# From the third batch on, q times k^T v as four plain float32 matmuls, one per quadrant of the array

## The chip, the cores and the metric

The kernel runs on one core of a Trainium2 chip. The time is device microseconds of one execution. The core has a matmul engine (PE in the rows, with its weight loads as PEld), a vector engine (DVE), a scalar engine (ACT), a general engine (POOL) and a queue that issues the transfers (SP). Each engine works through its own instructions in program order.

## What is computed

Eight batches of linear attention with eight heads, an RMS norm over each head, and a feed-forward block with a SiLU gate on all tokens:

```python
kv  = np.einsum('bhsd,bhse->bhde', k, v)          # 64 x 64 for each head
out = np.einsum('bhsd,bhde->bhse', q, kv)
rms = np.sqrt(np.mean(out * out, axis=-1, keepdims=True) + 1e-06)
x   = (out / rms * g_norm)                        # 4608 tokens x 512
h   = x @ w_in                                    # 512 x 2048
y   = (h * (1.0 / (1.0 + np.exp(-h)))) @ w_out    # 2048 x 512
```

Batch 8, heads 8, sequence 576, head dimension 64, everything in float32.

## The kernel before

The feed-forward block is nearly all the work. It runs over nine tiles of 512 tokens. Each operand there is split into an upper part that the array takes whole (type `fp32r`) and the rest, and a product is three matmuls: lower times upper, upper times lower, upper times upper. Tiles 0 and 1 are plain; from tile 2 on seven block products take the place of eight, for which sums of weight blocks are made on the way, written to DRAM and loaded back each step (`load_sums`, tile `wi<-sums_in_dram`).

Attention of batch b is woven into the feed-forward steps of earlier tiles. A batch is four pairs of heads (`Pair`), so 128 partitions hold two heads of 64. The place of every piece is written out by hand: `STAGES[b]` gives, in thirds of a step, when a pair's k and v are loaded (`load_kv`), when k^T v is made (`kv`), when q is loaded, split, multiplied (`out`, two thirds per pair: one for each half of its 576 columns), summed, scaled and kept. Third n belongs to step n // 3 and to its first, middle or last jobs by n % 3. Since every engine keeps program order, this list is also the order on each engine.

For a pair, `split_q` makes `qh` (ACT, L396) and `ql` (POOL, L401) out of `q`. All these tiles, with k and v, come from one pool of eight buffers (`kvq`), so a load of the next batch waits until an older tile of the ring is released. k^T v of the four pairs stands in one bank; `upper_kv` (ACT) copies it to `kh` and `lower_kv` (DVE) puts the rest in `kl`, both block-diagonal with zeros outside, so that one 128 x 128 weight tile serves both heads. `mm_out` then makes one half of the columns, 256 or 320 of them, by three matmuls (L414, L415, L416) in one bank. The banks for this are two, taken in turn (`at_bank`, tags `at` and `other`). `copy_out` empties a bank by two ACT instructions: the square (L420) and the scaled copy (L421).

The sums of weight blocks for the seven products are made between these: `make_sums` adds and subtracts on DVE (L691, L694), casts on ACT (L699), subtracts on POOL (L700) and stores. `move_a22` is one more ACT copy (L746). `spread` and `scale` of the batch before are on DVE (L434, L442).

Of the kernel before, what the change touches and what calls it, by code (L numbers as in the profile page):

```python
# [8 lines left out]
F32 = mybir.dt.float32  # L9
F32R = mybir.dt.float32r  # L10
# [29 lines left out]
        "load_q": (42, 42, 42, 48),  # L40
        "upper": 42,
        "lower": 43,
        "split": (46, 51, 54, 57),
        "out": (52, 53, 55, 56, 58, 59, 61, 62),
        "sums": (54, 57, 62, 63),
        "root": ((63, 6), (64, 5), (65, 3), (66, 4)),
# [6 lines left out]
        "load_q": (66, 66, 66, 72),  # L53
        "upper": 66,
        "lower": 66,
        "split": (70, 73, 76, 79),
        "out": (76, 77, 78, 80, 82, 83, 85, 86),
        "sums": (78, 81, 85, 87),
        "root": ((88, 6), (89, 4), (89, 4), (90, 4)),
# [6 lines left out]
        "load_q": (91, 93, 93, 99),  # L66
        "upper": 91,
        "lower": 92,
        "split": (97, 98, 103, 106),
        "out": (101, 102, 104, 105, 107, 108, 110, 111),  # L70
        "sums": (103, 106, 109, 112),
        "root": ((112, 6), (114, 4), (115, 4), (116, 4)),
# [6 lines left out]
        "load_q": (114, 114, 114, 120),  # L79
        "upper": 114,  # L80
        "lower": 115,
        "split": (118, 118, 121, 127),
        "out": (124, 125, 127, 129, 131, 132, 134, 135),
        "sums": (126, 129, 132, 135),
        "root": ((136, 7), (138, 4), (139, 4), (140, 3)),
# [6 lines left out]
        "load_q": (138, 138, 138, 144),  # L92
        "upper": 138,
        "lower": 139,
        "split": (142, 145, 148, 151),
        "out": (148, 149, 151, 152, 154, 155, 157, 158),
        "sums": (151, 154, 157, 160),
        "root": ((160, 6), (161, 4), (162, 4), (163, 4)),
# [6 lines left out]
        "load_q": (162, 162, 162, 168),  # L105
        "upper": 162,
        "lower": 163,
        "split": (166, 171, 172, 175),
        "out": (172, 173, 175, 176, 178, 179, 181, 182),
        "sums": (174, 177, 180, 183),  # L110
        "root": ((187, 7), (188, 4), (189, 3), (190, 4)),
# [20 lines left out]
def linear_attention_rms_silu_ffn(  # L132
# [22 lines left out]
    nc = tc.nc  # L155
    B, NP, P, S = q.shape
    D = P // 2
# [11 lines left out]
    const = ctx.enter_context(tc.tile_pool(name="const", bufs=1))  # L169
# [14 lines left out]
    def gap(pool, size, name):  # L184
        pool.tile([P, size // 4], F32, name=name, bufs=1)
# [8 lines left out]
    gap(const, 128, "gap_first")  # L194
    gap(tmp, 192, "gap_tmp")
    gap(gp, 64, "gap_gated")
    kh, kl = (const.tile([P, NP, P], F32R, name=name) for name in ("kh", "kl"))
    ident = weights.tile([P, P], F32, name="ident", tag=f"wo{EARLY}")
    make_identity(nc, ident)
    first_kv = weights.tile([P, NP * P], F32, name="first_kv", tag=f"wo{EARLY - 1}")  # L200
# [151 lines left out]
    def newton(y, u, m, eps=0.0):  # L352
# [4 lines left out]
            lambda: nc.vector.scalar_tensor_tensor(out=y, in0=u, scalar=1.5, in1=y, op0=ALU.add, op1=ALU.mult),  # L357
        ]

    class Pair:  # L360


# [24 lines left out]
        def split_q(self):  # L387

            self.qh = kvq.tile([P, S], F32R, name="qh", tag="kvq")
            self.ql = kvq.tile([P, S], F32R, name="ql", tag="kvq")  # L390
            cols = slice(0, S)
            if self.b == 1:
                cols, most = slice(TN, S), slice(0, TN)
                bank = h_bank() if self.c else at_bank()
                nc.scalar.copy(out=bank, in_=self.q[:, most])
            nc.scalar.copy(out=self.qh, in_=self.q)  # L396
            if self.b == 1:
                nc.vector.tensor_tensor(
                    out=self.ql[:, most], in0=bank, in1=self.qh[:, most].bitcast(F32), op=ALU.subtract
                )  # L400
            nc.gpsimd.tensor_tensor(  # L401
                out=self.ql[:, cols], in0=self.q[:, cols], in1=self.qh[:, cols].bitcast(F32), op=ALU.subtract
            )

        def begin_out(self):
            self.sq = tmp.tile([P, S], F32, name="sq", tag="tmp")
            self.o = opool.tile([P, S], F32, name="o")
# [49 lines left out]
    class FirstPair(Pair):  # L457
# [10 lines left out]
        def copy_kv(self):  # L468
            for h in range(2):
                d = slice(h * D, (h + 1) * D)  # L470
                nc.scalar.copy(out=kvm[self.c][d, d], in_=self.kv[h])
# [124 lines left out]
    def h_bank():  # L596
        return ps_h.tile([P, 512], F32, name="hp", tag="h")
# [6 lines left out]
    def at_bank(tag=None):  # L604

        at_tags.append(at_tags.pop(0))
        return ps_at.tile([P, 512], F32, name="at", tag=tag or at_tags[-1])
# [32 lines left out]
    def sums_of(t):  # L640

        whole, half = slice(0, DM), (slice(0, DM // 2), slice(DM // 2, DM))
        banks = [(acc_bank(), n, whole) for n in range(TN // P)]
        if t == NT - 1:
            last, n, _ = banks.pop()
            banks += [(last, n, half[0]), (at_bank(), n, half[1])]
        return banks
# [632 lines left out]
    def at(jobs, step, *calls):  # L1280
        jobs.setdefault(step, []).extend(calls)

    def at_third(n, *calls):
        at((first_jobs, mid_jobs, last_jobs)[n % 3], n // 3, *calls)

    def spread_at(make, *places):

        calls = []
        for n, (third, count) in enumerate(places):
            def some(n=n, count=count):  # L1290
                if not n:
                    calls.extend(make())
                for _ in range(count):
                    calls.pop(0)()
            at_third(third, some)
# [4 lines left out]
    def plan(b, g):  # L1300

        ps = [Pair(b, c) for c in range(NP)]
        norms, kvs = [], []

        def begin():
            norms[:] = [small.tile([P, NP, S // 32], F32, name=name) for name in ("sums", "y")]

        def out_half(p, half):
            p.mm_out(half)
            p.copy_out()  # L1310

        def kv_block():

            kvs.append(at_bank())
            kv_of(ps)

        def kv_of(some):
            for p in some:
                p.mm_kv(kvs[0][:, p.c * D:(p.c + 1) * D], range(4), start=p.c == 0)
            for p in some:  # L1320
                p.mm_kv(chunks=[4], stop=p.c == NP - 1)

        def kv_begin():

            kvs.append(at_bank())
            kv_of(ps[:-1])

        def by_head():
            kv = kvs[0][:, :NP * D].rearrange("p (c d) -> p c d", d=D)
            return [(kv[d], kh[d, :, d], kl[d, :, d]) for d in (slice(0, D), slice(D, P))]  # L1330

        def upper_kv():
            for kv, to, _ in by_head():
                nc.scalar.copy(out=to, in_=kv)

        def lower_kv():
            for kv, upper, to in by_head():
                nc.vector.tensor_tensor(out=to, in0=kv, in1=upper.bitcast(F32), op=ALU.subtract)

        if b == 1:  # L1340
            at(last_jobs, g, kv_block)
            at_third(3 * g + 3, upper_kv)
            at_third(3 * g + 3, lower_kv)
        else:
            places = STAGES[b]
            for p, third in zip(ps, places["load_kv"]):
                at_third(third, lambda p=p: p.load(which="kv"))
            if b == 2:
                at_third(places["kv"], kv_block)
            else:  # L1350
                at_third(places["kv"], kv_begin)
                at_third(places["kv"] + 2, lambda: kv_of(ps[-1:]))
            for p, third in zip(ps, places["load_q"]):
                at_third(third, lambda p=p: p.load(which="q"))
            later = 0 if b == 2 else 2
            at_third(places["upper"] + later, upper_kv)
            at_third(places["lower"] + later, lower_kv)
        for p in ps:
            half = [lambda p=p, i=i: out_half(p, i) for i in range(2)]
            sums = lambda p=p: p.sum_sq(norms[0][:, p.c])  # L1360
            if b == 1:
                split_at, first_at, second_at, sums_at = SECOND[p.c][:4]
            else:
                split_at, sums_at = (places[kind][p.c] for kind in ("split", "sums"))
                first_at, second_at = places["out"][2 * p.c:2 * p.c + 2]
            at_third(split_at, p.split_q)
            at_third(first_at, p.begin_out, half[0])
            at_third(second_at, half[1])
            at_third(sums_at, *[begin] * (p.c == 0), sums)
        spread_at(lambda: rsqrt(*norms, b == 1), *(SECOND_ROOT if b == 1 else places["root"]))  # L1370
        for p in ps:
            if b == 1:
                scale_at, cast_at = SECOND[p.c][4:]
                at_third(scale_at, lambda p=p: p.spread(norms[1][:, p.c], 0), lambda p=p: p.scale(0))
                at_third(cast_at, lambda p=p: p.to_tile(0))
                at(mid_jobs, NF + 1 + p.c, lambda p=p: p.spread(norms[1][:, p.c], 1), lambda p=p: p.scale(1))
            else:
                for part in (0, 1) if b == 2 else (None,):
                    at_third(
                        places["x"][p.c], lambda p=p, part=part: p.spread(norms[1][:, p.c], part),  # L1380
                        lambda p=p, part=part: p.scale(part)
                    )
                at_third(places["keep"][p.c], p.keep)
        return ps

    with tc.manual_schedule():

        first = [FirstPair(c) for c in range(NP)]
        stats = at_bank()
        g_stats, stats = stats[:, 256:257], stats[:, :64].rearrange("p (c i j) -> p c i j", i=2, j=8)  # L1390
        second = plan(1, AT[1])
        for item in ORDER.split():
            kind, n = item.rstrip("0123456789"), int(item.lstrip("wiopbgq") or 0)
# [162 lines left out]
        for t in range(NT):  # L1556
            if t < OUT7:
                sums = sums_of(t)
# [90 lines left out]
```

## Time and profile before

| | |
|---|---|
| median of 3 runs | 798.6 us (796.83 to 799.57) |
| profiled execution, first to last instruction | 798.8 us |
| PE busy | 786.2 us, 98% |
| DVE, ACT, POOL busy | 77%, 53%, 31% |
| granted TensorE clock, mean | 0.997 |

The profile covers one execution from its first to its last instruction. What lies around that span is not in it, and no time of its own is given for this execution, so its span is set beside the runs' times: it is 0.2 us above their median. A matmul shows as a record on PE and one on PEld; a plain float32 matmul shows as two of each. Starts of records are measured, ends are modelled, so lengths of work on PE are read from start to start.

### The profile page before, as it was taken

To read this page: it belongs to the slowest core of one execution; us is meant where nothing else is said; L and a number is where in the kernel's file an instruction comes from. 1 tells how busy PE (TensorE), PEld (TensorE's weight loads), DVE (VectorE), ACT (ScalarE), POOL (GpSimd) and SP (SyncE) were. 2 spreads that over 40 slices of the span, in tenths; PEclk is the share of its full clock that TensorE was granted. 3 is DMA by queue.
4 is the path that set the end of the run, shared out by engine and by line. 5 is a ranking of instruction groups with operands and counts; after the bars stand their busy time and mean duration, and the time that the engine had idled before them with its cause. 6 is when DMAs were issued, how large, how long until landed. Compare 5 with 4: busy or idle time off the path is not lost.

```text
span 798.8 us, 18542 instructions
## 1 busy us (share of the span) xinstructions
PE 786.2 (98%) x7242; PEld 779.0 (98%) x7242; DVE 614.1 (77%) x1244; ACT 425.5 (53%) x876; POOL 246.5 (31%) x282
## 2 busy tenths in 40 slices
PE   8999999999999999989999999999999999999997
PEld 7899999999999999989999999999999999999997
DVE  5999986689866889747876688778867886788666
ACT  4888465437464456644644455445644654465443
POOL 2799684555555518437241000000000000000001
PEclk9999999999999999999999999999999999999999
DMA  9994024546498675875558866765676567657653
GB/s 344 415 415 146 1 61 152 190 164 235 178 319 287 218 274 188 305 251 174 188 204 297 277 230 202 253 219 185 220 252 225 197 225 249 210 200 221 208 185 119
DMA packets 91962, 177.37 MB, mean 222 GB/s; under 512 B 8675, under 2 KB 52707, under 8 KB 91875
## 3 DMA queue, kind: packets, MB, share of 16 engines
q1 hardware_dynamic: 91874, 176.19, 64.0%
q8 instruction: 57, 0.93, 0.5%
q14 instruction: 31, 0.25, 0.1%
HBM read 143.66 MB, written 32.51 MB: 221 GB/s over the span
## 4 chain that ended last, share of the span: by engine, by line
PE 91%; POOL 2%; issue 2%; DVE 2%; DMA 2%; ACT 1%; SPq 0%; DVEq 0%; POOLq 0%; ACTq 0%
PE hp L829 33%; PE acc L614 20%; PE acc L1002 13%; PE hp L614 9%; PE at L1002 7%; PE hp L1002 3%; PE at L382 2%; DMA wi<-sums_in_dram 1%; PE at L414 1%; PE at L415 1%; PE at L416 1%; DMA early_wo<-in_v 1%; POOL wi L322 1%; POOL wo L322 0%; POOL x_second L455 0%
## 5 line engine op out<-in xcount | busy, mean ns | idle before, releaser
L614 PE MATMUL acc<-wo,gh 128*128 128x256 f32 x1024 | 161.5, 277 | 0.0
L829 PE MATMUL hp<-x_second,wi 128*128 128x256 f32 x1152 | 149.7, 277 | 0.0
L829 PEld LDWEIGHTS hp<-x_second,wi 128*128 128x128 f32 x1152 | 139.7, 188 | 0.1
L614 PEld LDWEIGHTS acc<-wo,gh 128*128 128x128 f32 x1024 | 137.1, 188 | 0.5
L948 ACT ACTIVATE gated<-gated 128x512 f32<-128x512 f32 x80 | 50.6, 633 | 121.7 <-DVE gated L1240 91.1
L1058 POOL TENSOR_TENSOR ob<-ob,e 128x256 f32<-128x256 f32 x1 | 0.7, 739 | 367.8 <-ACT ob L1061 367.8
L829 PE MATMUL hp<-operand,wi 128*128 128x256 f32 x864 | 112.1, 277 | 2.1 <-DMA wi<-sums_in_dram 2.1
L829 PEld LDWEIGHTS hp<-operand,wi 128*128 128x128 f32 x864 | 104.6, 188 | 2.6 <-issue 2.3
L614 PE MATMUL acc<-wo,gl 128*128 128x256 f32 x512 | 99.8, 276 | 0.0
L614 PEld LDWEIGHTS acc<-wo,gl 128*128 128x128 f32 x512 | 77.2, 188 | 0.0
L1002 PE MATMUL acc<-wo,gh 128*128 128x256 f32 x320 | 58.5, 276 | 0.0
L1002 PE MATMUL acc<-s,gs 128*128 128x256 f32 x360 | 53.7, 276 | 0.0
L401 POOL TENSOR_TENSOR ql<-q,qh 128x576 fp32r<-128x576 f32 (+1 forms) x28 | 38.4, 1373 | 45.6 <-ACT qh L396 25.2
L1002 PEld LDWEIGHTS acc<-wo,gh 128*128 128x128 f32 x320 | 48.2, 188 | 0.0
L1225 ACT COPY gated<-hp 128x256 f32<-128x256 f32 x40 | 14.9, 372 | 61.8 <-PE hp L829 61.8
L614 PE MATMUL hp<-x_second,wi 128*128 128x256 f32 x384 | 46.7, 277 | 0.2 <-POOL x_second L455 0.2
L1002 PEld LDWEIGHTS acc<-s,gs 128*128 128x128 f32 x360 | 46.7, 188 | 0.0
L614 PEld LDWEIGHTS hp<-x_second,wi 128*128 128x128 f32 x384 | 45.1, 188 | 0.5 <-POOL x_second L455 0.4
L614 PE MATMUL hp<-x,wi 128*128 128x256 f32 x360 | 44.6, 278 | 0.8 <-POOL x L562 0.8
L1002 PE MATMUL acc<-wo,gl 128*128 128x256 f32 x160 | 44.2, 276 | 0.0
L961 DVE TENSOR_TENSOR wi<-gated 128x256 f32<-128x256 f32 x80 | 33.9, 424 | 13.4 <-ACT gated L948 12.0
L954 DVE TENSOR_TENSOR gl<-gated,gh 128x384 fp32r<-128x384 f32 x80 | 43.9, 549 | 0.0
(227 smaller groups left out, 1841.6 us busy)
## 6 DMA issues: line engine op xcount, KB each, us to landing
wi<-sums_in_dram SPq DMA_DIRECT2D x112, 512.0 KB, 3.7
s<-out_sums SPq DMA_DIRECT2D x120, 256.0 KB, 4.6
wi<-in_moe_w_in SPq DMA_DIRECT2D x16, 512.0 KB, 7.8
wo<-in_moe_w_out SPq DMA_DIRECT2D x16, 512.0 KB, 8.9
sums_in_dram<-sum_parts SPq DMA_DIRECT2D x16, 512.0 KB, 2.9
out_sums<-wi SPq DMA_DIRECT2D x16, 512.0 KB, 3.1
k<-in_k SPq DMA_DIRECT2D x28, 288.0 KB, 4.3
v<-in_v SPq DMA_DIRECT2D x28, 288.0 KB, 4.5
```

The source lines that it names most:

```text
L322: nc.gpsimd.tensor_tensor(out=w[:, 1, :], in0=full, in1=w[:, 0, :].bitcast(F32), op=ALU.subtract)
L382: nc.tensor.matmul(out=self.kv[h], lhsT=self.k[rows, c, :], rhs=self.v[rows, c, :], start=(start and r == 0), stop=(stop and r == 4),)
L401: nc.gpsimd.tensor_tensor(out=self.ql[:, cols], in0=self.q[:, cols], in1=self.qh[:, cols].bitcast(F32), op=ALU.subtract)
L414: nc.tensor.matmul(out=ps, lhsT=upper, rhs=self.ql[:, w], start=True, stop=False)
L415: nc.tensor.matmul(out=ps, lhsT=lower, rhs=self.qh[:, w], start=False, stop=False)
L614: nc.tensor.matmul(out=to[:, at:at + 256], lhsT=stationary, rhs=moving[:, at:at + 256], start=start and at == 0, stop=stop and at == n - 256,)
L829: nc.tensor.matmul(out=out, lhsT=a_of(i, a, c), rhs=x[b][:, c], start=start and n == 0, stop=n == 5, skip_group_check=not check,)
L948: nc.scalar.activation(out=self.gated, in_=self.gated, func=AF.Silu)
L954: nc.vector.tensor_tensor(out=self.plain[1], in0=self.gated[:, P:], in1=self.plain[0].bitcast(F32), op=ALU.subtract)
L961: nc.vector.tensor_tensor(out=f[:, 0:2], in0=y[:, 1:3], in1=y[:, 0:1].to_broadcast([P, 2, P]), op=ALU.subtract)
L1002: nc.tensor.matmul(out=self.out[m], lhsT=g[m], rhs=self.weight(m, j, a), start=j == 0 and n == 0 and m in self.opens, stop=j == HF - 1 and ...
L1225: nc.scalar.copy(out=first.gated[:, low], in_=u)
```

## The change

From batch 2 on (the third) q is no longer split and k^T v no longer has an upper and a lower part. The host lays q out so that partitions 0 to 63 hold the first 288 columns of both heads and partitions 64 to 127 the other 288. k^T v of both heads is copied to both partition halves of one float32 tile: ACT copies each head to its own half, DVE to the other one. A pair is then four plain float32 matmuls of 64 rows, 64 weight columns and 288 moving columns, one for each combination of partition half and head; the two partition halves write to two banks, which are both taken at the place where the first half was made before. The place of the second half only empties the second bank. The places themselves are as they were. Batches 0 and 1 are not touched.

```diff
-        "split": (70, 73, 76, 79),          # this line goes in every stage
         "out": (76, 77, 78, 80, 82, 83, 85, 86),
...
+    def kv_twice(b):
+        if b not in twice:
+            name = ("kh", "kl")[b % 2]
+            twice[b] = const.tile([P, NP, P], F32, name=f"kv_twice{b}", tag=name)
+        return twice[b]
...
+        def mm_quadrants(self):
+            n = S // 2
+            self.banks = [at_bank()[:, :n] for _ in range(2)]
+            for r in range(2):
+                rows = slice(r * D, (r + 1) * D)
+                for h in range(2):
+                    nc.tensor.matmul(
+                        out=self.banks[r][h * D:(h + 1) * D, :], lhsT=kv_twice(self.b)[rows, self.c, h * D:(h + 1) * D],
+                        rhs=self.q[rows, h * n:(h + 1) * n], start=True, stop=True,
+                    )
+
+        def empty_quadrants(self, half):
+            n = S // 2
+            self.w, self.ps = slice(half * n, (half + 1) * n), self.banks[half]
+            self.copy_out()
...
+        def copy_kv(on_scalar):
+            kv = kvs[0][:, :NP * D].rearrange("p (c d) -> p c d", d=D)
+            halves_ = slice(0, D), slice(D, P)
+            for h, d in enumerate(halves_):
+                r = h if on_scalar else 1 - h
+                (nc.scalar.copy if on_scalar else nc.vector.tensor_copy)(
+                    out=kv_twice(b)[halves_[r], :, halves_[h]], in_=kv[d]
+                )
...
-                split_at, sums_at = (places[kind][p.c] for kind in ("split", "sums"))
+                sums_at = places["sums"][p.c]
                 first_at, second_at = places["out"][2 * p.c:2 * p.c + 2]
-            at_third(split_at, p.split_q)
+                half = [lambda p=p: p.mm_quadrants() or p.empty_quadrants(0), lambda p=p: p.empty_quadrants(1)]
+            if b == 1:
+                at_third(split_at, p.split_q)
             at_third(first_at, p.begin_out, half[0])
             at_third(second_at, half[1])
```

## Rows read from the trace of the kernel before

**Rows 1.** The page: busy time by engine, and the chain by engine

```profile
PE 786.2 (98%) x7242; PEld 779.0 (98%) x7242; DVE 614.1 (77%) x1244; ACT 425.5 (53%) x876; POOL 246.5 (31%) x282
...
PE 91%; POOL 2%; issue 2%; DVE 2%; DMA 2%; ACT 1%; SPq 0%; DVEq 0%; POOLq 0%; ACTq 0%
```

**Rows 2.** Timeline of PE, batch 3: start us, us, what, [idle before <-releaser]

```profile
172.53 0.28 PE L414 MATMUL at<-ql,kh 128*128 128x256 f32 x1
...
172.88 0.63 PE L614 MATMUL acc<-wo,gh 128*128 128x256 f32 x4
...
181.86 0.31 PE L414 MATMUL at<-ql,kh 128*128 128x320 f32 x1
...
182.29 2.89 PE L614 MATMUL hp<-x_second,wi 128*128 128x256 f32 x24
```

**Rows 3.** Timeline of PE: plain float32 matmuls of 128 columns on the whole array

```profile
13.51 0.61 PE L1408 MATMUL hp<-ident 128*128 128x128 f32 x4
13.96 1.06 PE L477 MATMUL acc<-first_kv,early_wo 128*128 128x128 f32 x8
```

**Rows 4.** Timeline of PE: plain float32 matmuls on parts of the array

```profile
22.16 0.49 PE L490 MATMUL acc<-ident,on 128*128 128x128 f32 x3
22.58 0.32 PE L506 MATMUL at<-first_kv,early_wo 128*64 128x128 f32 x1
22.58 0.32 PE L506 MATMUL at<-first_kv,early_wi 128*64 128x128 f32 x1
...
23.16 0.50 PE L614 MATMUL acc<-x,wi 128*128 128x256 f32 x2
...
344.82 0.56 PE L382 MATMUL at<-v,k 64*64 64x64 f32 x12
```

**Rows 5.** Timelines of PE, ACT, POOL and DVE around batch 3's first two pairs

```profile
176.04 0.28 PE L414 MATMUL at<-ql,kh 128*128 128x256 f32 x1
...
179.59 0.63 ACT L699 CAST sum_parts<-sums 128x512 fp32r<-128x512 f32 x1 [3.52 <-DVE sums L694]
...
180.64 0.43 ACT L420 ACTIVATE sq<-at 128x320 f32<-128x320 f32 x1
180.97 0.52 ACT L421 ACTIVATE o<-at,gcol 128x320 f32<-128x320 f32 x1
...
176.43 1.74 POOL L401 TENSOR_TENSOR ql<-q,qh 128x576 fp32r<-128x576 f32 x1
...
171.18 0.36 DVE L442 TENSOR_TENSOR o<-o,yT 128x192 f32<-128x192 f32 x1
...
177.21 1.18 DVE L442 TENSOR_TENSOR o<-o,yT 128x192 f32<-128x192 f32 x1
```

**Rows 6.** Timelines of ACT and PE, batch 6, first and second pair

```profile
323.15 0.54 ACT L421 ACTIVATE o<-at,gcol 128x320 f32<-128x320 f32 x1
...
323.10 0.28 PE L414 MATMUL at<-ql,kh 128*128 128x256 f32 x1
```

**Rows 7.** Timeline of PE, and windows: length, busy (records) by engine, PEclk, DMA share, GB/s

```profile
345.32 1.65 PE L829 MATMUL hp<-operand,wi 128*128 128x256 f32 x12
349.09 1.25 PE L829 MATMUL hp<-operand,wi 128*128 128x256 f32 x6 [2.12 <-DMA wi<-sums_in_dram]
...
349.00:351.00 2.00, 1.91 (x11) 1.94 (x12) 0.00 (x0) 0.00 (x0) 1.59 (x6) 0.63 0.74 288
351.00:353.00 2.00, 2.00 (x23) 1.55 (x22) 0.76 (x2) 0.89 (x2) 2.00 (x3) 0.52 0.08 32
```

**Rows 8.** Timelines of the transfer queue SP and of PE, batch 6's last pair

```profile
333.19 0.38 SPq L371 DMA_DIRECT2D v<-in_v  x1
339.68 0.33 SPq L371 DMA_DIRECT2D k<-in_k  x1
...
341.11 0.90 SPq L758 DMA_DIRECT2D wi<-sums_in_dram  x2
...
334.90 0.28 PE L414 MATMUL at<-ql,kh 128*128 128x256 f32 x1
```

More of the change, by code (lines that the diff above doesn't have):

```diff
@@ L42 @@
         "lower": 43,
-        "split": (46, 51, 54, 57),
         "out": (52, 53, 55, 56, 58, 59, 61, 62),
@@ L68 @@
         "lower": 92,
-        "split": (97, 98, 103, 106),
         "out": (101, 102, 104, 105, 107, 108, 110, 111),
@@ L81 @@
         "lower": 115,
-        "split": (118, 118, 121, 127),
         "out": (124, 125, 127, 129, 131, 132, 134, 135),
@@ L94 @@
         "lower": 139,
-        "split": (142, 145, 148, 151),
         "out": (148, 149, 151, 152, 154, 155, 157, 158),
@@ L107 @@
         "lower": 163,
-        "split": (166, 171, 172, 175),
         "out": (172, 173, 175, 176, 178, 179, 181, 182),
@@ L196, in linear_attention_rms_silu_ffn @@
     gap(gp, 64, "gap_gated")
-    kh, kl = (const.tile([P, NP, P], F32R, name=name) for name in ("kh", "kl"))
+    kh, kl = (const.tile([P, NP, P], F32R, name=name, tag=name) for name in ("kh", "kl"))
     ident = weights.tile([P, P], F32, name="ident", tag=f"wo{EARLY}")
@@ L358, in newton @@
         ]
+    twice = {}
+    def kv_twice(b):
[3 more added lines that the diff above has]
+        return twice[b]
     class Pair:
@@ L1330, in by_head @@
             return [(kv[d], kh[d, :, d], kl[d, :, d]) for d in (slice(0, D), slice(D, P))]
+        def copy_kv(on_scalar):
[6 more added lines that the diff above has]
+                )
         def upper_kv():
+            if b > 1:
+                copy_kv(True)
+                return
             for kv, to, _ in by_head():
@@ L1336, in lower_kv @@
         def lower_kv():
+            if b > 1:
+                copy_kv(False)
+                return
             for kv, upper, to in by_head():
@@ L1622, in lay_out @@
             b, h, s, d = a.shape
-            a = a.transpose(0, 1, 3, 2).reshape(b, h // 2, 2 * d, s)
+            whole = a[:2].transpose(0, 1, 3, 2).reshape(2, h // 2, 2 * d, s)
+            split = a[2:].reshape(b - 2, h // 2, 2, 2, s // 2, d).transpose(0, 1, 3, 5, 2, 4)
+            a = np.concatenate([whole, split.reshape(b - 2, h // 2, 2 * d, s)])
         elif name in ("k", "v"):
```

## The prediction

> **What bounds the kernel now.** I read the page first: PE is busy for 786 of 798.8 us, and 91% of the chain that ended last is PE [rows 1]. So an edit moves the time in two ways: it changes how long PE needs for the same products, or it makes PE wait. ACT, DVE and POOL have room on average, and work taken from them is worth nothing unless PE waits for it somewhere. Second, the timeline of PE around a pair, for its present price [rows 2]. Third, the places where the trace already has plain float32 matmuls and matmuls on parts of the array, since the new form has both [rows 3, 4]. Fourth, ACT beside PE at every place where a pair follows a pair, because the new form needs both banks at once [rows 5, 6]. Last, the longest wait of PE after the first 25 us, and the queue that caused it [rows 7, 8].
>
> **What PE does for a pair.** Before, the first half takes 172.88 - 172.53 = 0.35 us and the second 182.29 - 181.86 = 0.43 us, 0.78 us in all [rows 2]. It is ordinary work in a full stream, without a gap.
>
> The new price has two terms. The stream: four plain float32 records of 128 columns take 13.96 - 13.51 = 0.45 us, 0.112 us each [rows 3]. At the granted 2.4 GHz, 128 columns are 0.053 us, so each record streams its columns twice, with 5 ns over; and a matmul is two records (eight for the four products of a pair in the first batch). A matmul of 288 columns is then 2 x (2 x 288 / 2400 + 0.005) = 0.49 us, an estimate from that row. How many of the four run at a time decides. Two that use different halves of the columns start within a hundredth of a microsecond of each other [rows 4], and so do two that differ in rows and columns: twelve records of 64 columns, streamed twice, would be 12 x 0.053 = 0.64 us in turn, and the row has all of them in 0.56 us with the last one's 0.2 us of tail [rows 4]. Two that share columns and differ in rows are nowhere in this trace. From below, all four together cost 0.49 us; from above, two and two cost 0.98 us. I take 0.49, since both forms that the trace has run side by side, each tile with a stream of its own.
>
> The second term is going into parts of the array and back. The group at L506 stands between full matmuls. The three before it, 0.49 us with a tail of 0.27, start every 0.11 us, so a fourth would have started at 22.49. The two after it start at 23.16 and take 0.50 where two need 0.39 (0.28 and one step of 0.11), so the stream is level again as if from 23.27. Of these 0.78 us, four steps of 0.112 are the stream (eight records, two at a time); 0.33 us is the price of the change of shape [rows 3, 4]. So a pair costs 0.49 + 0.33 = 0.82 us instead of 0.78: 0.04 us more, 24 pairs, **+1.0 us**. The saving of the four-fold array is just eaten by entering and leaving it.
>
> The Trainium skill has this in two places. "TensorEngine Tiling (Array Packing)", Key Properties, says that a change of tiling mode drains the array; the 0.33 us agree. "TensorE: Matmul & The Clock Gate", Part 3, gives the span of packed tiles as one matmul's duration and some 4 ns for each further tile, with no charge for the change; by that the sum here would be -6.9 us instead of +1.0. The row decides for the charge. The same part reports tiles in different row groups as concurrent, which no row here shows.
>
> **What leaves the other engines.** One ACT cast and one POOL subtraction per pair are gone, and `lower_kv` becomes a copy that no longer waits for ACT. The two kv copies come at least seven thirds before the first pair needs them, so they lie beside feed-forward products. I cost all this at nothing, except where it changes a wait below. The squares and scaled copies are the same columns in other halves.
>
> **The added wait.** `mm_quadrants` writes both banks at the first place. So the matmuls of a pair wait until ACT has emptied the *second* bank of the pair before, where until now only the first bank had to be free. PE keeps order: everything behind waits too. In batch 3 the second half of pair 0 is emptied at third 77 and pair 1 starts at third 78, with no PE work between. ACT is late there: it stands for 3.52 us before the cast at 179.59, which waits for DVE's sums, and the square and copy of the second half come only at 180.64 and end at 181.49 [rows 5]. PE was at pair 1 at 176.04 [rows 5]. With the longer pairs of batch 2 and pair 0 that is 176.2. From above, the wait is 181.5 - 176.2 = 5.3 us. DVE gets faster: its 192-column product took 1.18 us beside POOL's `ql` where the same one took 0.36 without [rows 5], and one more `ql` stands earlier in this stretch. That gives 0.8 to 1.6 us back; with 1.4, ACT is done at 180.1. The first two matmuls go ahead meanwhile, so the loss is 180.1 - 176.3 = 3.8 us, of which PE stands idle for 3.3. From below I take 2.5.
>
> After an idle stretch of that length the clock falls. The trace has one: after 2.1 us of waiting the granted clock was 0.63 and 0.52 of 2.4 GHz in the next two windows of 2 us, its lower level of 1.2 GHz, which loses 2 x (0.37 + 0.48) = 1.7 us [rows 7]. So this place costs 3.8 + 1.7 = **+5.5 us** (2.5 to 7.0).
>
> Elsewhere pairs are further apart or ACT is in time. At the first step of batch 6 ACT ends at 323.69 and the next pair starts at 323.10 [rows 6]: 0.6 us, unless the cast that is gone moves ACT ahead by as much. Batch 5 looks alike. I take 0.6 for both, **+0.6** (0 to 1.2).
>
> **The wait that may go.** At 347 PE ran out of work and waited 2.12 us for `sums_in_dram`, then lost 1.7 at the low clock: 3.8 us [rows 7]. That load was issued at 341.11, after the queue had stood still from 333.57 to 339.68 before the last k of batch 7 [rows 8]: it needed a buffer of `kvq` that held the last pair's split q, until the matmuls of third 158. Without `qh` and `ql` the ring turns 12 tiles in a batch instead of 20; that k needs the buffer of pair 2's q, and only the v behind it waits, for the last pair's matmuls at third 157, which is 334.90 [rows 8]. So the load can go out near 336, five microseconds earlier. What is late next is the transfer itself: it took eight microseconds under load (341.11 to 349.09), and 336 + 8 is before 347. **-3.8 us** (0 if the transfers ahead of it hold it back).
>
> **The sum.** 798.8 + 1.0 + 5.5 + 0.6 - 3.8 = 802.1 us, made against the profiled execution, whose span is 0.2 above the median of 798.6. I say 802.
>
> **The rivals.**
> Row halves take turns: the four matmuls run two and two, a pair costs 0.49 more, 24 x 0.49 = 11.8, and the time is 814. For it: no row shows two tiles in the same columns. Against it: every other combination runs side by side. Chance 0.16.
> The sums still come late at 347: 806, since the 3.8 us are not won. For it: that transfer took eight microseconds although the queue had stood still before it [rows 7, 8]. Chance 0.17.
> Not slower: ACT is in time in batch 3, so the wait there does not exist. It decides at ACT's second copy ending before 176.3, for which DVE's sums must come five microseconds earlier than they did; without the casts on ACT and the subtractions on POOL a part of that is given. Then 798.8 + 1.0 + 0.6 - 3.8 = 796.6, or 800.4 if the sums wait stays. Chance 0.12.
> No charge for the change of shape: were the tiles of a pair loaded under the stream before them, each pair would cost 0.49 and 24 x 0.33 = 7.9 us would go: 794. Against it stands the 0.33 us of L506. Chance 0.04. That is the span rule of "TensorE: Matmul & The Clock Gate" in the Trainium skill.
>
> **How the numbers follow.** The forecast case (four at a time, the wait in batch 3, the sums in time) has 0.5 and reaches from 798 to 805 by its bounds. With the late sums at 806 and their upper bounds, and with ACT in time at 796.6, the range 796 to 809 holds some 0.8; the case of turns lies above and the case without a charge below. A difference of 0.3%, 2.4 us, is about what a measurement of this kernel can tell from no change. Faster than 796.2: the case without a charge and under half of the case of ACT in time, 0.09. Between 796.2 and 801: the rest of that case and the lower end of the forecast, 0.17. Slower: 0.74.
>
> **What would show it.** Four PE starts within some 0.03 us at each `mm_quadrants`, and 0.82 us from the full matmul that would have come to the level stream behind; a spacing of the second two half a microsecond later would be the turns. At the second pair of batch 3 a gap of about 3 us that ACT's copy ends, with the granted clock near 0.5 behind it. No gap before L829 near 350, and the load of the sums issued five microseconds sooner. The prediction is wrong if that gap is missing, if the row halves take turns, or if a later transfer takes the place of the one at 347.

## The result, and the profile after

The changed kernel takes 805.58 us (median of 5 runs, 804.74 to 808.7), the kernel before 798.47 us beside it (796.83 to 799.57). The ratio is 1.0103, with a 95% interval of 1.0085 to 1.0121: 7.1 us slower by the medians. The forecast was 802, so +3.4. The sign was right, but less than half of the loss was forecast.

The page of the kernel after, its first line:

```profile
span 803.0 us, 18547 instructions
```

The executed time of this profiled execution is on record: 804.74 us, 1.7 us over its span. That difference, 1.7 to 1.8, comes back in every profiled run below. So the profiled execution of before, with its span of 798.8, was one of about 800.5 us, 2 us above the median, and not the typical one that the prediction took it for.

The waits of PE, kernel after: who waited <- for whom, us in total, times, longest.

```profile
PE at L415 <- ACT o L442: 3.1, 1, 3.1
```

A new wait of 3.1 us for ACT stands at the four matmuls (L415), and the wait of 2.12 us for `sums_in_dram` [rows 7] is gone: no such line is left. Both were forecast. The timeline of PE, kernel after (start us, us, what, [idle before <-releaser]):

```profile
121.23 1.64 PE L635 MATMUL hp<-x_second,wi 128*128 128x256 f32 x13
122.80 0.72 PE L415 MATMUL at<-q,kv_twice 64*64 64x288 f32 x8
123.44 0.50 PE L635 MATMUL acc<-wo,gh 128*128 128x256 f32 x2
...
176.70 0.70 PE L415 MATMUL at<-q,kv_twice 64*64 64x288 f32 x4
180.47 1.20 PE L415 MATMUL at<-q,kv_twice 64*64 64x288 f32 x4 [3.07 <-ACT o L442]
...
330.26 1.53 PE L415 MATMUL at<-q,kv_twice 64*64 64x288 f32 x8
...
343.00 0.72 PE L415 MATMUL at<-q,kv_twice 64*64 64x288 f32 x8
...
351.34 2.11 PE L385 MATMUL at<-v,k 128*64 128x64 f32 x60
```

Four things are read here. First, two of the four matmuls alone (four records, at 176.70) take 0.70 us, and all four (eight records, at 122.80) take 0.72: they run at the same time. Second, the price of a usual pair. The thirteen full matmuls before it end at 122.87, the last one's record 0.28 long, so a fourteenth would have started 0.11 after that one's start, at 122.70. The two full ones behind it take 0.50 where two need 0.39 (0.28 and a step of 0.11), so the stream is level as if from 123.55. That is 0.85 us; before it was 0.78 [rows 2]. Third, batch 3: the first two matmuls of pair 1 start at 176.70, the other two 3.77 us later. Fourth, batch 6's pair 1 at 330.26: eight records take 1.53 us and not 0.72, and the list of waits has nothing of it.

The timeline of ACT in the same stretch of batch 3, and at batch 6's pair 1, kernel after:

```profile
178.58 0.62 ACT L720 CAST sum_parts<-sums 128x512 fp32r<-128x512 f32 x1 [3.19 <-DVE sums L715]
...
179.63 0.40 ACT L441 ACTIVATE sq<-at 128x288 f32<-128x288 f32 x1
179.93 0.49 ACT L442 ACTIVATE o<-at,gcol 128x288 f32<-128x288 f32 x1
...
330.54 0.51 ACT L442 ACTIVATE o<-at,gcol 128x288 f32<-128x288 f32 x1
```

ACT stands 3.19 us before the cast of DVE's sums (3.52 before [rows 5]) and empties pair 0's second bank at 180.42, five hundredths before PE goes on. In batch 6 the second bank is empty at 330.54 + 0.51 = 331.05, 0.79 us after pair 1 began at 330.26: its first two matmuls run alone for 0.70 us meanwhile, so the profile shows PE busy, but the last two could not run beside them. The 192-column product on DVE that took 1.18 us beside `ql` [rows 5] takes 0.36 now:

```profile
177.02 0.36 DVE L463 TENSOR_TENSOR o<-o,yT 128x192 f32<-128x192 f32 x1
```

The windows around the wait, kernel after: stretch, length, then busy us (instructions) of PE, PEld, DVE, ACT and POOL, granted clock, DMA share, GB/s.

```profile
180.00:182.00 2.00, 1.53 (x6) 0.67 (x7) 1.97 (x3) 1.63 (x5) 1.56 (x2) 0.64 0.31 125
182.00:184.00 2.00, 2.00 (x11) 2.00 (x11) 1.93 (x3) 0.00 (x0) 0.27 (x1) 0.51 0.95 365
184.00:186.00 2.00, 2.00 (x20) 2.00 (x20) 0.00 (x0) 0.27 (x1) 0.00 (x0) 1.00 1.06 274
```

After the wait the granted clock falls to its lower level, 1.2 GHz, for some 3.4 us: 2 x (0.36 + 0.49) = 1.7 us lost, as the 1.7 in [rows 7].

The transfer queue SP at the last pair of batch 6, kernel after:

```profile
344.18 4.18 SPq L779 DMA_DIRECT2D wi<-sums_in_dram  x2
```

The load of the sums goes out 1.2 us after the last pair's matmuls (343.00 in PE's timeline); before, 341.11 - 334.90 = 6.2 us after [rows 8]. The queue comes free five microseconds sooner, as forecast. The load is two transfers, and that holds for the first; the second goes out at 348.04.

**Where the 7 us arose.** A stretch of the program is measured by two marks: the starts of the k^T v blocks, whose second block of one batch and first block of the next lie on either side of that batch's pairs. The timelines of PE, only the k^T v blocks that bound batches 3, 5 and 6; kernel after:

```profile
155.70 0.95 PE L385 MATMUL at<-v,k 128*64 128x64 f32 x20
209.10 2.11 PE L385 MATMUL at<-v,k 128*64 128x64 f32 x60
...
259.66 0.95 PE L385 MATMUL at<-v,k 128*64 128x64 f32 x20
302.92 2.11 PE L385 MATMUL at<-v,k 128*64 128x64 f32 x60
307.90 0.95 PE L385 MATMUL at<-v,k 128*64 128x64 f32 x20
```

and another profiled execution of the kernel before (run before_third below):

```profile
156.41 0.95 PE L382 MATMUL at<-v,k 128*64 128x64 f32 x20
204.31 2.11 PE L382 MATMUL at<-v,k 128*64 128x64 f32 x60
...
255.41 0.95 PE L382 MATMUL at<-v,k 128*64 128x64 f32 x20
297.77 2.11 PE L382 MATMUL at<-v,k 128*64 128x64 f32 x60
302.76 0.95 PE L382 MATMUL at<-v,k 128*64 128x64 f32 x20
345.14 2.11 PE L382 MATMUL at<-v,k 128*64 128x64 f32 x60
```

Batch 3 takes 53.40 us instead of 47.90, batch 5 43.26 instead of 42.36, and batch 6 (to 351.34 in the timeline above) 43.44 instead of 42.38. The four pairs of a batch are 0.25 of each by their shape (e2 below, which has no wait). What is left over is 5.2 us in batch 3, 0.6 in batch 5 and 0.8 in batch 6. In batch 6 it is the wait for the second bank, in batch 3 that wait and the low clock behind it. In batch 5 the late bank is only 0.1 of it, in this execution. PE in batch 5, kernel after:

```profile
282.02 0.83 PE L415 MATMUL at<-q,kv_twice 64*64 64x288 f32 x8
...
285.00 2.28 PE L850 MATMUL hp<-x_second,wi 128*128 128x256 f32 x18
```

The group of pair 1 takes 0.83 us instead of 0.72. The other 0.5 us are a slower stream: from 283 to 298 the full matmuls start every (2.28 - 0.28) / 17 = 0.118 us, against (1.64 - 0.28) / 12 = 0.113 in the row at 121.23, with the granted clock at 1.00 in both. What slows them is not shown. The second profile of the same kernel (after_again below) has no such stretch there, but a wait of 1.31 - 0.72 = 0.6 us:

```profile
283.81 1.31 PE L415 MATMUL at<-q,kv_twice 64*64 64x288 f32 x8
```

### The profile page after: what moved, and what is told of

It reads as the page before. It is cut to its first block, busy times and chain, and to the rows that moved or that the text cites. A ratio compares the mean times of both kernels' runs of the same rounds, so it can differ in the third digit from the quotient of the medians.

```text
span 803.0 us, 18547 instructions
## 1 busy us (share of the span) xinstructions
PE 789.4 (98%) x7290; PEld 767.5 (96%) x7290; DVE 602.9 (75%) x1244; ACT 413.2 (51%) x852; POOL 207.0 (26%) x258
## 4 chain that ended last, share of the span: by engine, by line
PE 74%; DVE 3%; ACT 1%; DMA 1%; issue 0%; DVEq 0%; ACTq 0%
PE hp L850 33%; PE acc L635 13%; PE acc L1023 13%; PE at L1023 6%; PE hp L1023 3%; PE hp L635 2%; PE at L415 2%; PE at L385 1%; DMA out<-ob 1%; DVE sums L715 0%; DVE yT L455 0%; DVE wi L985 0%; DVE upper L712 0%; DVE x L1079 0%; DVE x L463 0%
## 5 line engine op out<-in xcount | busy, mean ns | idle before, releaser
L635 PEld LDWEIGHTS hp<-x,wi 128*128 128x128 f32 x360 | 42.3, 188 | 1.2 <-POOL x L583 1.0
```

Source lines behind the costliest of these rows:

```text
L635: nc.tensor.matmul(out=to[:, at:at + 256], lhsT=stationary, rhs=moving[:, at:at + 256], start=start and at == 0, stop=stop and at == n - 256,)
```

## The experiments

The theory: the loss is one wait in batch 3 (with the low clock behind it), two small ones in batches 5 and 6 and a small charge for the shape; what the shorter ring gives back is much less than the 3.8 us forecast, since the 2.12 us wait is not in every execution of before. The rivals: the quadrants themselves are dear (shape, not wait); the wait comes from the removed casts rather than from taking both banks at once; and the ring's 3.8 us are won in full, something else being lost.

**The kernel before, profiled again.** No edit.

> The kernel before, unchanged, profiled and timed again. The wait theory says that the 2.1 us wait for sums_in_dram near 349 us and the low clock after it (3.8 us together) belonged to the one execution that was profiled: a new profile of a usual execution has a span near 796.7 us and no gap of PE over 1 us after 25 us; the times stay near 798.5 us. The rival, that this wait is in most executions and the changed kernel really won 3.8 us there, expects the same gap of about 2 us near 349 us again and a span near 798.8 us.

Measured: 799.14 us, ratio 1.0008 [0.9977, 1.0038], span 796.5. The waits of PE in it:

```profile
PE hp L829 <- DMA wi<-sums_in_dram: 0.6, 1, 0.6
PE hp L829 <- DVE gf L883: 0.5, 1, 0.5
```

The wait for `sums_in_dram` is 0.6 us here, in another batch (at 231.7), and none stands near 349; the mean granted clock is 0.999. A third profile:

> The kernel before, unchanged, once more, five rounds beside the others. Both theories: times near 799 us that spread over some 6 us. If the waits for sums_in_dram come and go (theory A), this third profile shows none, or one at another place than 349 us, and a span between 795 and 799 us. If the wait near 349 us is a lasting part of the kernel (theory B), it is there with 1 us or more.

799.29 us, 1.0002 [0.9987, 1.0017], span 797.6, with one such wait of 0.5 us, at 232.8. So over three executions of one kernel such waits cost 3.8 us (with the low clock), 1.1 (0.6 for the sums and 0.5 for DVE) and 0.5: they vary, and the prediction rested on the largest.

Why there is no wait near 349 can be read too. The queue in this third profile, at the last k of batch 7:

```profile
341.55 0.33 SPq L371 DMA_DIRECT2D k<-in_k  x1
...
343.19 0.90 SPq L758 DMA_DIRECT2D wi<-sums_in_dram  x2
```

and how long the two loads of 341.11 [rows 8] and the two of 343.19 took to land, first the one execution, then the other:

```profile
DMA to landing us min/median/max: 7.8/8.3/8.7
```

```profile
DMA to landing us min/median/max: 5.3/6.0/6.7
```

The queue had stood still here as well, from 335.67 to 341.55, and the load went out 343.19 - 336.77 = 6.4 us after the last pair's matmuls, as late as the 6.2 of [rows 8]. In before_again it is 6.6. But the first load landed after 5.3 us (4.5 in before_again) and not after 7.8, and PE found it there. So the late load is in all three executions and the wait in one: what made the difference was the length of the transfer.

**e1: pair 0's second bank of batch 3 is emptied one third earlier.** Everything else is as in the kernel after.

```diff
-        "out": (76, 77, 78, 80, 82, 83, 85, 86),
+        "out": (76, 76, 78, 80, 82, 83, 85, 86),
```

> The changed kernel with one number changed: in batch 3 the second bank of the first pair is emptied at the place of the first one (third 76 instead of 77), ahead of the ACT cast that waits for DVE. Wait theory: the 3.07 us gap before the second pair of batch 3 and the low clock after it go, 5.2 us less than the changed kernel, about 800.4 us. Rival (the change of shape costs more than the 0.85 us that the starts show, spread over all 24 pairs, or work given to other engines later costs it): at most 2 us less, 803.5 us or more, with PE gaps elsewhere.

Measured: 799.87 us, ratio 0.9998 [0.9977, 1.0019]; in a second set of runs

> The variant with the second bank of batch 3's first pair emptied at the first place, five rounds. Both theories: no gap of PE over 0.3 us between 30 and 400 us in its profile, 799 to 800 us. Against the kernel before on this chip: theory A (the ring of buffers is no part of the matter) +1.6 us for the shape of the array; theory B (the shorter ring saves the waits for sums_in_dram) +1.6 less 3.8, so 2 us below.

800.04 us, 1.0015 [0.9999, 1.0032]. ACT and PE in batch 3, first of the two runs:

```profile
174.93 0.53 ACT L442 ACTIVATE o<-at,gcol 128x288 f32<-128x288 f32 x1
177.96 0.62 ACT L720 CAST sum_parts<-sums 128x512 fp32r<-128x512 f32 x1 [2.50 <-DVE sums L715]
```

```profile
176.08 0.72 PE L415 MATMUL at<-q,kv_twice 64*64 64x288 f32 x8
```

The second bank's copy now stands ahead of the cast that waits for DVE; it ends at 175.46, pair 1 starts at 176.08 and does not wait. ACT still stands 2.50 us before the cast, but nothing that PE needs is behind it. One number takes back nearly the whole loss, with all 24 pairs still as quadrants: the loss is the wait, not the quadrants.

**e2: the second bank is emptied at the first place in every batch from 2 on.**

```diff
-            at_third(second_at, half[1])
+            at_third(second_at if b == 1 else first_at, half[1])
```

> The changed kernel with the second bank of every pair from batch 2 on emptied at the place of the first one. Wait theory: besides the 5.2 us of batch 3 the small waits of batches 5 and 6 (about 0.6 us together) go; what is left over the kernel before is 24 x 0.065 = 1.6 us for the shape, about 800 us. Rival as for the single number: 803 us or more.

799.98 us, 1.0001 [0.9979, 1.0023]. Again, in a later set of runs:

> The changed kernel with every second bank emptied at the first place, five rounds. The wait theory has 1.6 us for the shape over an undisturbed execution of the kernel before and nothing else, and saves 1.4 us in batches 5 and 6 against the variant that does so in batch 3 alone: 798.6 to 799.5 us, no gap of PE over 0.1 us between 120 and 400 us. Rival (the ring of buffers brings nothing, so the kernel before stays 1.6 us ahead in the median): 800.3 us or more.

798.19 us, 1.0008 [0.9994, 1.0022]. The k^T v blocks around batches 5 and 6, second run:

```profile
254.27 0.95 PE L385 MATMUL at<-v,k 128*64 128x64 f32 x20
296.89 2.11 PE L385 MATMUL at<-v,k 128*64 128x64 f32 x60
301.88 0.95 PE L385 MATMUL at<-v,k 128*64 128x64 f32 x20
344.50 2.11 PE L385 MATMUL at<-v,k 128*64 128x64 f32 x60
```

Both batches take 42.62 us, 0.25 more than before: the shape of four pairs, and no wait. With every wait of the quadrants gone, the shape still costs 6 x 0.25 = 1.5 us, yet the time ties with before at +0.6 us (-0.5 to +1.8). So some 0.9 us (-0.3 to 2.0) come back in a usual execution, by the shorter ring or by the lighter load of ACT, POOL and DVE; no run tells them apart. e1 keeps the waits of batches 5 and 6, 1.5 us in its second profile; its expectation left them out, and so its +1.2 looks as if nothing came back. With them the same sum gives 1.8 (0.4 to 3.1) by its second set of runs and some 3 by its first. The second sets of both shut out the 3.8 forecast; 1.5 lies within what they allow.

**e3: the wait without the quadrants.** The kernel before, its two halves made at the first place and emptied at the two places.

```diff
+        def mm_both(self):
+            made = []
+            for i in range(2):
+                self.mm_out(i)
+                made.append((self.w, self.ps))
+            self.made = made
...
+                half = [lambda p=p: p.mm_both() or p.empty_made(0), lambda p=p: p.empty_made(1)]
```

> The kernel before with its split q and its six matmuls per pair, but with both halves multiplied at the first place, so that both banks are taken at once, and the second bank emptied at the second place as in the changed kernel. It has the wait without the quadrants. Wait theory: a gap of 3 to 5 us before the second pair of batch 3, ended by ACT, with the low clock after it: 804 to 806 us. Rival (the quadrants themselves cost the time): 798.5 us, no gap.

Measured: 807.27 us, ratio 1.0097 [1.0062, 1.0133]. PE in batch 3:

```profile
178.47 0.28 PE L414 MATMUL at<-ql,kh 128*128 128x256 f32 x1
...
183.93 0.63 PE L414 MATMUL at<-ql,kh 128*128 128x320 f32 x1 [4.96 <-ACT o L432]
```

Taking both banks at one place costs as much by itself as the whole change does. The gap is 4.96 us, against 3.07 with the quadrants. From the pair's start to the work in its second bank it is 183.93 - 178.47 = 5.46 us, against 3.77: without `qh` and `ql` ACT is done 1.7 us nearer to PE (the prediction had 0.8 to 1.6 and took 1.4). The rival that blames the removed casts falls.

**e6: the gap of batch 3 filled.** Between the first two and the last two matmuls of that pair stand 28 matmuls of 224 columns whose output nothing reads; that work is added to what the kernel computes.

```diff
-            self.banks = [at_bank()[:, :n] for _ in range(2)]
+            wide = [at_bank() for _ in range(2)]
+            self.banks = [bank[:, :n] for bank in wide]
...
+                if r and (self.b, self.c) == (3, 1):
+                    for _ in range(28):
+                        nc.tensor.matmul(
+                            out=wide[0][:, n:512], lhsT=parts["wi", 3][:, 0, 0:P], rhs=x_second[:, 0, 0, 0:512 - n],
+                            start=True, stop=True,
+                        )
```

> The changed kernel with 28 matmuls of 224 columns that nothing reads, put between the first two and the last two matmuls of batch 3's second pair, so that PE works through most of the wait. The wait itself stays. Low-clock theory: of the 5.3 to 6.7 us that this place costs, what goes beyond the wait of 3 us is the low clock after it; with work in the gap the granted clock stays at 1.0 there and 1.7 to 3.4 us come back, less some 0.3 for one more change of shape: 803 to 804.5 us. Rival (the clock doesn't matter, the place costs because everything behind it is late): 805.6 to 806.1 us as the changed kernel, or 0.3 more.

Measured: 803.61 us, 1.0065 [1.0052, 1.0078]. The timeline of PE, and the window behind the gap:

```profile
177.67 3.39 PE L417 MATMUL at<-x_second,wi 128*128 128x224 f32 x28
180.98 0.70 PE L422 MATMUL at<-q,kv_twice 64*64 64x288 f32 x4
```

```profile
182.00:184.00 2.00, 2.00 (x20) 2.00 (x19) 1.97 (x3) 0.00 (x0) 0.62 (x1) 1.00 0.92 351
```

PE is late by as much as before (the last two matmuls start 180.98 - 177.04 = 3.94 us after the first two, against 3.77), but the clock stays at 1.00, where the kernel after has 0.51. Batch 3 takes 52.00 us (156.04 to 208.04) against 53.40, 1.4 less, although the added matmuls bring one more change of shape, some 0.3 us by e7 below. So of the 5.2 us there about 1.7 is the low clock and about 3.6 the wait. The prediction had 1.7 and 3.8.

**The kernel after, profiled again.** No edit.

> The changed kernel, unchanged, on the same chip as the others, so that it stands against the single-number variant directly: 5.2 us above it by the wait theory, with the gap of about 3 us before the second pair of batch 3 in this profile too; if that gap had been a matter of one execution, 1 us above it.

806.14 us, 1.0093 [1.007, 1.0117]; again a gap of 3.07 us at the same place. Windows of it:

```profile
182.00:184.00 2.00, 2.00 (x10) 2.00 (x11) 1.97 (x3) 0.00 (x0) 0.38 (x1) 0.50 0.95 363
184.00:186.00 2.00, 2.00 (x12) 2.00 (x11) 0.07 (x1) 0.00 (x0) 0.00 (x0) 0.50 0.99 292
186.00:188.00 2.00, 2.00 (x16) 2.00 (x16) 0.00 (x0) 0.84 (x2) 0.00 (x0) 0.78 1.00 321
```

The same gap, but here the clock stays low for 6.8 us and batch 3 takes 54.75 us (155.80 to 210.55): the wait costs 6.6 us and not 5.2. What decides how long the clock stays low was not found.

**e5: the ring made long again.** e1, and each pair takes two more tiles of the `kvq` ring, held by a one-column fill on POOL and released by a one-column copy on ACT; both are added work.

```diff
+            if half == 0:
+                self.held = [kvq.tile([P, S], F32, name=name, tag="kvq") for name in ("held0", "held1")]
+                for t in self.held:
+                    nc.gpsimd.memset(t[:, 0:1], 0.0)
+            else:
+                for t in self.held:
+                    nc.scalar.copy(out=warm_up, in_=t[:, 0:1])
```

> The same variant with two more tiles of the ring per pair, taken at the first place by a one-column write and held by a one-column read at the second, so that the ring turns 20 tiles in a batch again and the next batch's loads wait as in the kernel before. It adds two small instructions on POOL and two on ACT per pair. Theory B: the queue SP stands for some 6 us before the last k of batch 7, waits for sums_in_dram come back, and the time rises by 2 to 4 us over the same variant with the short ring. Theory A: SP stands there too, but the time rises by under 0.7 us.

Measured: 817.02 us, 1.0235 [1.0208, 1.0262]. Waits in it:

```profile
POOL held L428 <- PE at L385: 53.6, 4, 20.0
...
PE hp L857 <- DVE gf L911: 4.5, 2, 2.4
```

The holders themselves did this: POOL stood for up to 20 us before a fill, ACT stood for POOL, and PE for DVE behind them. No wait for `sums_in_dram` shows. The run tells neither theory and was inconclusive.

**e7 and e8: one block of k^T v instead of two, with the short ring and with the long one.** The last pair's k^T v stands in a block of its own two thirds after the other three, for want of its k and v. e7 is e2 with one block; e8 is the kernel before with the same edit.

```diff
-                at_third(places["kv"], kv_begin)
-                at_third(places["kv"] + 2, lambda: kv_of(ps[-1:]))
+                at_third(places["kv"] + 1, kv_block)
```

> The variant with all second banks emptied early, and k^T v of batches 3 to 7 made in one block a third after the old first place, instead of three pairs and the last pair two thirds later. It saves five excursions to parts of the array. Shape theory: an excursion costs what it did in the kernel before, 0.33 us for the change and 0.15 for going from 128 to 64 rows, so 5 x 0.49 = 2.4 us less than without this edit, about 796 us, 0.3% ahead of the kernel before. Rival (the change of shape is hidden or cheaper than the starts show): no change, 798.2 us. If the last pair's k and v land too late at the new place, PE waits there for a transfer instead.

> The same edit alone on the kernel before, whose ring of buffers turns 20 tiles in a batch. Ring theory: the last pair's k and v come some 3 to 6 us later there, so PE waits for them at k^T v of batch 5 or 7 and the 2.4 us are lost again or turned into a loss: 798 us or more. Rival (the ring does not matter): 2.4 us less than the kernel before, about 796 us.

e7 takes 796.57 us, ratio 0.9977 [0.9962, 0.9991], and so is 0.2% faster than the kernel before and 1.2% faster than the kernel after. e8 takes 800.14 us, 1.0026 [1.0002, 1.005]. PE in e7:

```profile
205.97 2.70 PE L385 MATMUL at<-v,k 128*64 128x64 f32 x80
208.60 3.01 PE L635 MATMUL hp<-x_second,wi 128*128 128x256 f32 x24
```

and the waits of PE in e8:

```profile
PE at L382 <- DMA v<-in_v: 1.1, 1, 1.1
...
PE hp L829 <- DMA wi<-sums_in_dram: 0.4, 1, 0.4
```

With the long ring a v of batch 5 comes 1.1 us late for the single block, and PE stands 0.9 us for DVE in two other places; with the short ring no transfer is waited for. The block takes 2.63 us to the next full matmul. In e1's second run the two blocks of that batch take 205.42 - 203.38 = 2.04 and 209.24 - 208.37 = 0.87, 2.91 in all: one change of shape less saves 0.28 us, or 1.4 us over five batches. The expectation had 0.49 and 2.4; the ratios of e7 and of e2's second runs differ by 0.3%, 2.5 us with some 1.6 to either side, which decides for neither. The edit alone gains nothing on the old ring, and gains on the new one. That much the times show. That it is the transfers, early enough for another order, is read from one profile of each; that a wait of this kind is in every execution of e8 was not shown.

## Why the prediction was right and wrong

**The shape of a pair.** Right in kind: the four matmuls run at the same time (0.70 us for two, 0.72 for four), so the case of turns, 814, fell. The price is 0.85 us and not 0.82, and by batches 0.25 us for four pairs, so +1.5 instead of +1.0. The case without a charge fell too. The Trainium skill, "TensorE: Matmul & The Clock Gate", Part 3, has tiles in different row groups run concurrently, and the trace after agrees; its span rule, without a charge for the change of shape, does not: by an estimate from it a pair would be 0.50 us (-6.7 us in all, with the 4 ns for each further tile that the prediction's -6.9 leaves out), and the run has 0.85. e7's 0.28 us for one change less speaks for the charge too.

**The wait in batch 3.** Right in place, cause and size. Predicted: ACT done at 180.1, a gap of 3.3, the clock at its lower level for 1.7 us more, 5.5 in all. Measured: 180.42, 3.07, and 5.2 us in one execution, 6.6 in the other where the clock stayed low for 6.8 us; that the clock's share came out at 1.7 in the first is in part luck. What DVE gave back was 1.7 us and not 1.4, with PE at the pair half a microsecond later than reckoned. e1 removes it with one number, e3 makes it without the quadrants, e6 separates wait and clock. The case of ACT in time (796.6) fell: DVE's sums let ACT go on 1.0 us sooner (the cast at 178.58 and not at 179.59), 1.7 against the start of pair 1 (176.70 and 176.04 [rows 5]), and five were needed.

**Batches 5 and 6.** Forecast 0.6 (0 to 1.2) for both. The late banks cost 0.9 us (0.1 and 0.8) in the first profile and 1.4 (0.6 and 0.8) in the second, so the size was low and the bound just missed in one of them. In batch 6 the second bank is 0.79 us late and that is what it costs; the 0.59 worked out from before (323.69 - 323.10) was to stand for both batches, and batch 6 alone cost as much. The slower stream in batch 5 of the first profile, 0.5 us, was in no forecast. e2, which empties the banks earlier, has none of these waits.

**The wait that may go.** This step failed: "The wait that may go", -3.8 us. Its first half held: the queue comes free five microseconds sooner, and the load of the sums goes out 1.2 us after the last pair instead of 6.2. Its second half did not, that the late load costs the kernel before 3.8 us. The load was as late in the other two profiles of that kernel, landed after 4.5 and 5.3 us instead of 7.8, and PE did not wait for it; the 3.8 us were what one slow transfer cost in one execution. The other two lost 1.1 and 0.5 us to such waits, elsewhere. The mean of the three is 1.8, the runs give 0.9 to 3, and about 1.5 is my estimate. That the ring brings it is argued and not shown: no profile with the short ring (after, e1, e2, e6, e7) has a wait for `sums_in_dram`, but e3 and e5, with the long one, have none either.

With that the sum is 1.5 + 5.2 + 1.4 - 1.5 = 6.6 us, or 8.0 where the clock stays low longer; measured are 7.1 and, in the second set of runs, 0.0093 x 798.73 = 7.4. Of the 3.7 us between forecast and measurement, some 2.3 are this term, 0.8 batches 5 and 6 (with the slower stream), 0.5 the shape. The sum was also made against a span of 798.8 as if that were the time, while the time of an execution is its span and 1.7 us. By that the profiled execution was one of 800.5 us, above all three runs shown, and so held more waiting than usual. This came to light only with the result, which was the first to give a span and a time of one execution.

**Open.** Why the same load of the sums takes 4.5 us in one execution and 7.8 in another, what slows the stream of full matmuls by 4% in some stretches, and what decides how long the clock stays low after the same gap. What comes back against the kernel before is known to a microsecond at best, and whether the ring brings it was not shown.

## What to carry to other kernels

An edit that makes an instruction take two buffers at one place moves the deadline of whoever empties the second one; look up what that engine is waiting for between the two places, and move the emptying along with the taking (here one number was worth some 6 us). A wait that a single profile shows may belong to that execution alone: set its own time, not its span, against the runs, and count on such a wait only as far as a second profile has it. When a form needs fewer buffers, the gain may lie in an order that the transfers did not allow before, and that has to be made.

## What the runs showed of the hardware

The same gap of 3.07 us on PE was followed by 3.4 us at the lower clock in one execution and by 6.8 us in another. Full matmuls of 256 columns started every 0.118 us for 15 us of one execution, where another row of it has 0.113, at a granted clock of 1.00 in both; the other execution of the same kernel has no such stretch there. One load of the sums, sent out equally late in three executions, landed after 4.5, 5.3 and 7.8 us. Four plain float32 matmuls on the quadrants of the array run together, 0.72 us for all and 0.70 for two; where the second bank came 0.79 us late, the group took 1.53 us without an idle time that the list of waits shows: a wait of one half can lie hidden behind the other half's records. DVE's 192-column float32 product took 1.18 us while POOL subtracted [rows 5] and 0.36 when that was gone.
